# Loading k of the first nine pairs in whole rows and turning it by quarter products, with all operations in a new sequence

## The chip, the cores and the metric

The kernel runs on one core of a Trainium2 chip. A core has five engines that run side by side: TensorE (PE, matrix products), VectorE (DVE), ScalarE (ACT), GpSimd (POOL) and SyncE (SP, which here only issues DMAs). Sixteen DMA engines move data between HBM and the on-chip memory SBUF; PE writes its results to PSUM. The metric is the device time of one execution in microseconds (us); lower is better.

## The reference

All data is float32. Attention with normalised q and k on 8 batches x 12 heads, 448 tokens of 64 elements, is followed by a bilinear feed-forward block on the 3584 x 768 result, with 1536 inner columns.

```python
def rmsnorm(x, g):
    rms = np.sqrt(np.mean(x * x, axis=-1, keepdims=True) + 1e-06)
    return x / rms * g
q_n, k_n = (rmsnorm(q, g_q), rmsnorm(k, g_k))
scores = (1.0 / np.sqrt(64)) * np.matmul(q_n, k_n.transpose(0, 1, 3, 2))
attn = softmax(scores)
attn_out = np.matmul(attn, v)                       # (8, 12, 448, 64)
x = attn_out.transpose(0, 2, 1, 3).reshape(3584, 768)
out = ((x @ w_a) * (x @ w_b)) @ w_out
```

## The kernel before

**A pair.** The kernel treats four heads of one batch together: 24 such groups, which its code numbers p and which this text calls pairs, since each half of the 128 partitions holds two heads. Partitions 0 to 63 hold the first two heads, 64 to 127 the other two, and each partition holds 7 tokens of each of its heads (`NT` = 7).

**Loads.** q, k and v of a pair are 448 KB each, loaded by two DMAs on the SP queue (`loads`, L415). q and v are laid out so that each run in HBM is 7 tokens, 1,792 bytes. k is laid out with the two heads of a token side by side, so that each run is one token of one head, 256 bytes. For the very first pair the halves of q and k go by the SP and the ACT queue.

**Normalising.** ACT squares q and k (L462), DVE sums the squares (L464), POOL raises to the power -0.5 (L499). q is multiplied by its factor on DVE (L503), into a layout with the two heads of a token side by side; k isn't multiplied at all: its factor is the `scale` of the exponential, since the keys lie along the partitions of the scores (L594).

**Turning.** The products want q and k with the 64 elements of a head along the partitions. `turn_halves` (L525) turns a pair by 14 transposes on PE: for each of the 7 tokens and each half of the partitions, 64 rows x 128 columns against a 64 x 64 identity. ACT copies the result from PSUM (L548, L550). The first pair has its own copy of this in `turn_first`, between warm-up products that keep PE active.

**Attention.** For each of the 7 key blocks j of a pair there are four 64 x 64 x 448 score products (L588), two exponentials on ACT (L594), four value products (L610), and the sum over the keys: for the first four pairs by products with ones (L646), later by additions on DVE and POOL (L624) and one such product. The sums are inverted, spread by DMA and multiplied into the result (`invert`, `divide`). Scores, turned tiles and inverses share one PSUM tag, `sc`, with two buffers of two banks each.

**Weights.** At the same time the three weight matrices, which arrive as 64-bit floats, are rounded to float32 on DVE and ACT (`round_steps`, L247 to L256), combined into the factors of a fast matrix multiplication (L372), written back to HBM (`kept`), and streamed in again when they are used. Their loads of 768 KB a half and the writes go by the ACT queue (`hraw/n/h` and `lraw/n/h`: place n, half h).

**Feed-forward.** For two batches at a time there are first products (`quarter_products`, L1295; `deep_products`, L872) and last products (`last_product`, L996; `inner_products`, L1193). They begin while attention of later pairs is still running; up to about 225 us most of PE's work is attention, and attention of later pairs stands between feed-forward products after that.

**The order.** Every step is registered by `op(engine, us, key, emit, reads, writes, ...)` with a planned duration. `Plan.run` emits the 4,383 steps in the sequence that is stored, packed, in the string `ORDER`. Each engine then executes its own instructions in that sequence, and waits by semaphores for the data and the buffers of the others. `ORDER` alone decides what stands behind what; the durations in `op` are not used when the kernel is built.

```python
for w in range(2):
    pair = src[b, h0 + 2 * w:h0 + 2 * w + 2]
    nc.sync.dma_start(x[low_high[w]], pair.rearrange("h (p j) d -> p j h d" if nm == "k" else
                                                     "h (p j) d -> p h (j d)", j=NT))
...
nc.tensor.transpose(t[:, w, (j - j0) * D:(j - j0 + 1) * D], x[rows, j].rearrange("p h d -> p (h d)"), ident[rows, rows])
...
places = zlib.decompress(base64.b85decode(ORDER))
```

Of the kernel before, what the change touches and what calls it, by code (L numbers as in the profile page):

```python
# [12 lines left out]
FP32 = mybir.dt.float32  # L13
# [7 lines left out]
def _float_of(bits):  # L21
# [11 lines left out]
    "c-rkZ33OFOmba>2z4y1bzrW_^X9WZi2#d0afb@VOwk)Hl;0^%=5+ETV3JD;KU}OzzfUt>S6SF|r6PB<f5kWR-MYcw9qaDHNwx@ee-<JfTTYE-5"  # L33
    "<D8xztA4%r>ej8h)xEdw7dtU}6~u~YLMZWqYI@CpMNGpoOt0b(7{qAjRdnpCg1-egK!(^^o)~b03)}(cl;Gq5I3AtQrk|8;!dSy-k=3_FX7dNl"
    "jE8!{nfKGu(|Vp9K}MwZ0G13e2nNHzXP<*-pMmV0oXNX#VA8mWTfHkLY=+V|td*|=&o9Vdx(@y`bN%AXg@sV~1~?b2qzelmZ|Sn7B=65K5@ydD"
    "`G*nnVMgAZuVBWk+^e}uKZhlsuD+7H^3@fKSHiOM%Q(@O<ewEjIAeaW7S5=r3-eCGi8XZ2>#L!VxU1KY<$qpIVEM8?EZf_5@7HjB=e1qsuzmUg"
    "vg7KGt;V*Basj69DuqzVE+AW9K7+EA!YMd)@^~>EJ67Z@ehW6O1K7BB_XcstH+y&NfonT%FW<&V*;V*rJ3wg}S%F)Z7cJkk_2S!Sw{P=Qmz_C$"
    "x~%Nv;Z2nXkHOJ5;hjGo+51i9#yxxXUf;9lz=M0gtlWQf&wKkeR%|>`0p)LB{Al;?YB=0#{h^%)cOE#sVaNXc>-QhqcWB?ygOxEgl{NdS_nkis"
    "hqn7bEIVkF?XQGg@-EMwU2uIj?EGTK?>+;e<daWIoBXMyj9j_AWy_`Omo9C&^5vD^esS^h;)}(fd}^M*qMrZwf_(n+N3P2kN~KHZN<U-gzWDIN"
    "D<2mZfBb>^+m9}NbNSMx*rJQSDK2_%^Xapj&wWtzzFGAC`z7a#E_yB%U2v3~J$Lr#2Sr6kjvYT;bmGJ}CyyTg_oAAk*RCD;ebK)a)m#hzuI9^A"  # L40
    "XHI=qZGL*9>SR^%yN3@SK6?Jhx#RB~K6dnQO-<3M>i?)YRQ2xftE#K3e)H8=iPcr_)fClK7kzp{Ir!<pw<`7hZymjG0$|fID2K|8u=DiJ>XT4$"
    "ctyoKaHOLAdO4KuKGX!(9RR=+DuX?jYsxAvZYeqc(W=YmHm_3muPVXK%g+>-6a#U?_VrtrmTg#Dco5beT6=Kq7FYtGFW$Io$zoWy7>r8*^XHvg"
    "Na@@KbLYPYr`P2XI6env!K|4ubH>{axb|8u<i1L#PX~Zk046Iruw@clfC;V%<6%5xL-sg)7)I8ZEP%|6EK1YU(?_RMnl=guj7SAY84kmTnI?fD"
    "L$YDWU`l}ue2xG-^E5pD6g>4LJoN<9?%y9ChyIU3KX^p;JPduIZy)H>8=%)i@DLb10eZmwJ;;58bnk{rLDzfX-Y(FkGjt(_aW_B*Xy2|~2hx_@"
    "1#o8@fYz;`RZD1@1W7F{q}~*6Z%UdF()c!ebAv=kOn`)VNI=0O0MX%aI6|Xn=o}3NDS+R%9(-N^%LEg2T}J{shChHSCnpDTAbUbKj4Ob#OUH_1"
    "VeCsU6XTeWl{xk$@x_cW85zRpbPzCJ(JsPEFnsv%S94#5P1A>sXG2Axsi|2b(nqAF4jGY}vLrM0?a3J_DKH@|W%$Ao!(rawVZ#O|zmRMV88jFM"
    "4H`HBhUW|(n>-{r`MJTF$<GahLC@$<r#!0+8>a9%{P|e}h75R8?w>rM|6@;iwm<sh#77^0`0>a3Ir|NGq_4AY9~o`=i05HJ==Vb3K0@!_LhtUq"
    "9_rrx*Fw*3&paSW{hsL8PwLv$A@R<fcj?syI`!z%sZ;m+I(6&TrE{l_y*d_j?AYlZ;clTr_YU`U_*J)Gb?DZ$Lx(P1x^(E)`Cqzr?%c)Q{+{;5"
    "?skIaYUdK=QFn<BM@#X(=3?_^f^=^S-n0{M(vbs`SlhOY3D_Zt3X~ASY6m0|r~L)Ms67<4IEXm@1QZ0O5k_zH>&*L=5M^0G%1o0}%2e$PqcTHs"
    "*hFTCT;wq#uZ$MB5X*%?fH3A4m`S`AGwc*^cShDAJ5F_uSP?FS5f_mK!RP0K7cq&+bUL|?B~m7}VygBmHMI^JiVjg4vKTcjlTlqCcLVufkv`!D"  # L50
    "ZnEcL#I)Z5pC4(Ml$g4K(V!BrJ8BE4yw2imqu?V(V8KvOVE$%|d3|Un3v79HK~ah9`6CIt-QN)Mhp!2}CP{=T?CLm=fQ(4`sFd^+GGgRVl98H1"
    "&OA@Z3ull%9SqOHz-I<R)pJmF2o4;Cqm`#<B|Rio9o^gi$iDqGk5^RDYBXK{gP39;dAz|RpKPtzD(vRMmd(Pp507lyTw1od^u0c%rw$0ckN0`^"
    "UCuZ4dh^Y9Hg2ryCH(s9l9K)FcI<_s3bLWFCs|*zcIyLW7YbqZxgKkZ#Wia-t%g%;VCBkpw>j2seP{K`)hl0LxnkAw$`#8Gu2{Yf3f8SHcw>7("
    "VPRSKH!gQ8C94Q@UAbuWq7552EL*>>_rj%1dgmWmvaEDTe$~=d1#jik%EdH4zoKH^qTP!Z&Fc#DSHZlzy!Bg_u3NEe`Letvd2>!JUa~lU_1q<k"
    "7A;@2qNbqJvVvumuwX&{0+_#W{;q{H=WoAf9+bTXn`f8I&dpsg^X?gWuf8^S?wt8+U+*wGZ~EP{XHK7fctyd?yO&O*`7>$xjP`lcb6=S~dDhfU"
    "Q(h~5rFhDesne!SnmlQ0VPS_UbmHoct6rWsvE$V7ujEc?H)&e_<ViV`U(P9?H!*J#%bqZP{9O~qPtBp(lcsFUp1k4Z?1|Zh6S8x%?_9O&rLiks"
    "LXWv~OjcITm@(rPjUSgiu6*3MaWm%5p3!z@=8W7sGp4`Qdd!PilgEq^AZttpj7m?>O)vN;{l#hN`B|9@&y8*~|Lo{_X=$UzjvV=7){7&@jD%Ol"
    "W<u&{Ou8^JJtHkGJ$+BgsLZsK%(V23(Jj+zhF6b*W{?W0L!n8Np+lY@oG~~#Ic-#0@~Gsr5y`2kxRRQZGAOl4%D|!622Q&JQ{2Mrrt@#ZqNU-$"
    "CmK#1@N`2V^J#b@9TG<k7&%~g|6%=yCc?0Icp)L~`9Xsoj;DPYjXW7kAq?Tiq8`0JItoH02oUu5^grN7hi}ioYusrVos4?`OikB7#RyP6NuCxS"
    "k9xc3uG-uRs?#Z>Pewf4iJK(KIle4Vl?IA6M@dqB(Y~-@s#uh1c3oyErlzQk6%#8oElJZ=OH~Xdpdi4PWN5mMKYQvk_11=^D~6#271ghpdK>&S"  # L60
    "OhpZAilQ63ua&O&6(8=4G9rel>j7Q2n(J1SsR#YK?rnu2uVRD^O$n-oY50s5s%5FB8qou)r76A^hNdc-qG_tnr>m-_>Sl8#<X04>t%`J2#Ri4("
    "9W<5J$P<~F(a74T>rt&OpXD=j!wex`pVeA7{d$a1$4ynS0@W<7nWY#ZMGK(HN|NDI?7g_4`c|5%s<zbXX0{53)*59uBFGWh1vI;O^)*)_MwVqL"
    "5#5W3E&YbBgjLhjL)e3=sW&(9p{Qu8TG<q@(p2jaLIP+|%eJJYMJZ@It=7~nmF5QWS5?1VG`CTF8qxG<T~=fpL-r}M*OUXd%d)2V+gJuZHME&&"
    "XnsGcqG>I3*;J!cSqUp<$V^fUuW8AuEc+E%w(zaUs@~*nJy0#%`k)PyRM|k<NLsE{Pd0T~m(_@jy2+L-8_i?{g)~hzeP&BjAMI0RHH5}PbLlOK"
    "A*iZbSKW$$TwH$Q(VR|&Yuq8Z6N%x}Dfci@6&op{!{rb)Q4(cA;_`!{$R(Z2T!|$Ov_zuD$i(j<#N~ELnnWbQLs$bs;z?W_iH#*Z5{bkT5);9^"
    "9VF$UKwR5k=WvkvX=2N$=y0<@R3ID(#s>XyG(asPMWPHVK4{z#<fKW!AMkU(SB=DZ4a*97Rnrhqc81B{rxK5>Bzk1Gi9>NmC4}9E+anvqaw#so"
    "AtMeq@kq?$aJob$Nut*!d0pJ4aSfb_4H(|Cu}Tbg;6)}dPN;peVlflP1g9Xhvu|6014wvf;El^zD?(WV$wA{KDOM6&iP3UQOhAloFB0x2K{e?0"
    "JA77@6><>C%b1?Tn4uYx7IeyPh5(nt?O>`?a&YcW6kXh*q9I)(=ez-P36iJ^f-DFQy!9G!j)qo{B~v7KV~H~dHw;`u09Q~}hZ&CyMCRsNV;6Ty"
    "E{@yrl6NqN<Y*`fPQo}-P-cmX4MjIMIDSw}9}49f6&&`ZEJsV6y0Jc>tf4?T<%rI)5}~{i?z8V_g-X1!D7u|4&Z#8fT=1x>!_&ZFI9#Graymqm"
    "iJ~~1Q66z_r|!nog&j9bROEu2N^dwD+Qou{VIAV3RKn_{5i*kmB^MECQ$%!%q9jRzi1aCSGwPvk2i0RKRXH*i8*%Cs&}xbxaHp%^Z2~fNB2$qu"  # L70
    "50hMtBnj2#g2)6sL!{tDZgIAPD1wtZIBkfeMNU0+THS`#4T!p3z34<C=)#E>abdMURir9$;$cqal$ac0UvMWA8(oo@C^0lBMFrek^fVC7Q=*F!"
    "k;ojW2*j>67>{sLP9>Zm2Zk<SFHk4hh%V?7Xd+rxB}BICEDQoEo=BW4h{ZTZH%(v;DvAPk2~SanFo4w>j7At9&~OozN<<az$0OwEn7olFI$ciP"
    "wjxbp#6_Cd5w%^|L1|d@5Vw<<4zwB-o3%hwxCn8?6OusU;}c?HFc=*?j*!?G+!r8`kUu^?==1qnwD3iOcldpwCV?RFhW-91e=ryoxx?!V`(ymR"
    "C_l4&{@8e5j1`G^V=Sw46uZY~n*IQ>;z)vJ#bCF*x*0G7je?f!HMBUdnP3K@6HIC{B}yYvh8m=b;rA+*8Ba8~-xG~@j^<N>iHha5b1UX{J(Q#c"
    "v}T&p%&TZYs@*2UX?X9c_DvBoH5cYOOLgfk681SmYKY3j=i_dV*x2AMg9%!^lz`zA(n!D=#T`D@82zFlp1Ok8ry&|7B;Y233!|2?gct^(L`aB$"
    "1MgS|a06TdV4S&J0B+0%3`1YAGXU150tmI$soe<t!!`1~pFfQZ`GJgn)Y{)J{$wV0qdx|I3y{*AfZ9{7<%It{?7trNqjpN{K}hYR_6>G~*}oeD"
    ">`^-*b=Ws>Y2EHR2-Hn$G3&m`cWM6>i+UorF5PT@3!wGDdiHf(NWDT(&&UP|H}*oUgm6>BTS-IxraJj30J(MBw}i>JM!WeSH{j%!17zPl)bE4-"
    "X!ri-YV;=|&|6)Zeh(HpcYTA}QHMlpcimWn`pi}bruBHVo^pM>++3tLkiLc1%W;#}Up4qUaC(y&+z<<Ha;CS+@U1BHzqAScyIw-R3nV|qzsOJZ"
    "Q9}M3Wb#u&f&4)E$j==`KUZ9me^kMKY5!~q_WxxgKU*M?UxM<N_J2NC(Eo*aBmcv3@-s!(FG2fD`{C^`Cf^JG"
# [68 lines left out]
def kernel(  # L148
# [126 lines left out]
    def fast_body(ld, wk, ps_s, ps_o, ps_mm, dram):  # L275
# [8 lines left out]
        TURN = 0.42  # L284
# [130 lines left out]
        def loads(p, nm):  # L415
# [4 lines left out]
            def emit():  # L420
                x = ld.tile([P, NT, 2, D] if nm == "k" else [P, 2, NT * D], FP32, tag=nm, name=nm + "_sb", bufs=2 if nm == "v" else 1)
                for w in range(2):
                    pair = src[b, h0 + 2 * w:h0 + 2 * w + 2]
                    nc.sync.dma_start(x[low_high[w]], pair.rearrange("h (p j) d -> p j h d" if nm == "k" else
                                                                     "h (p j) d -> p h (j d)", j=NT))
                xs[nm, p] = x
            if p == 0 and nm != "v":
                def begin():
                    xs[nm, p] = ld.tile([P, NT, 2, D] if nm == "k" else [P, 2, NT * D], FP32, tag=nm, name=nm + "_sb", bufs=1)

                def half(w):
                    pair = src[b, h0 + 2 * w:h0 + 2 * w + 2]
                    queue[("SP", "ACT")[w]].dma_start(
                        xs[nm, p][low_high[w]], pair.rearrange("h (p j) d -> p j h d" if nm == "k" else "h (p j) d -> p h (j d)", j=NT))
# [4 lines left out]
            op("SP", 1.28 if nm != "k" else 1.4, p - (1.8 if nm == "v" else 2.0), emit, [f"firsts{PREP}"] if p >= HELD else [], [t], new=[t],  # L439
               kb={"q": 620, "k": 800, "v": 530}[nm], dmas=2)  # L440
# [4 lines left out]
        def normalize(p):  # L445
# [8 lines left out]
            def squares(s, nm):  # L454
                sq = tile_of(f"sq{nm}{p}", "sq", 1)

                def square():
                    x = xs[nm, p]
                    t = xs["sq", nm, p] = wk.tile([P, 2 * NT, D], FP32, tag="sq", name="sq")
                    flat = (x.rearrange("p h (j d) -> p (h j) d", d=D) if nm == "q" else  # L460
# [61 lines left out]
            qn = tile_of(f"qn{p}", "qn", 1)  # L522
            op("DVE", 1.15, key, apply, [f"{ms}/q", f"q{p}"], [qn], new=[qn], lock=True)

        def turn_halves(t, x, j0, j1):  # L525

            for j in range(j0, j1):
                for w in range(2):
# [1045 lines left out]
```

## Time and profile before

| | before |
|---|---|
| time, median of 3 runs | 1473.81 us |
| lowest and highest run | 1473.35 and 1478.22 us |
| profiled execution, its time | 1477.19 us |
| profiled execution, its span | 1475.2 us |
| PE busy | 1452.8 us, 98% of the span |
| DVE busy | 998.3 us, 68% |
| ACT busy | 438.1 us, 30% |
| POOL busy | 332.6 us, 23% |
| DMA packets | 188,884, of them under 512 bytes 62,564 |

The profile is of one execution, which took its own time; the median is of other executions. The span goes from the first to the last instruction. In the rows of a profile, L530 is line 530 of the kernel, PE is a product, PEld the load of a product's stationary operand, and names such as `pt<-ident,k_sb` are the tiles written and read. A row in square brackets names the idle time of the engine before the instruction and what ended it. "SPq" and "ACTq" are the instructions that issue DMAs. In the windows view the columns are the window, its length, busy time (and instructions) of PE, PEld, DVE, ACT and POOL, the granted share of the TensorE clock, the mean busy share of the DMA engines, and GB/s.

### The profile page before, as it was taken

The page shows a single profiled execution, that of the slowest core. Times are in us where ns is not written, and L with a number is a line of the kernel's source. Part 1 is how long each engine was busy: PE and PEld are TensorE (multiplying, and loading weights), DVE is VectorE, ACT ScalarE, POOL GpSimd, SP SyncE. Part 2 cuts the span into 40 slices and gives each one's busy share as a digit, 9 for nine tenths or more (in the row PEclk, how much of TensorE's full clock was granted, in tenths as well). Part 3 has the DMA queues.
Part 4 walks back from the last instruction along what each step waited for, and adds up shares of the span by engine and source line. Part 5 has one row for each costly group of instructions (what it writes and reads, how often), then busy time and mean ns, then how long its engine had stood idle before and what let it go on. Part 6 is the DMA issues. An engine that isn't in the chain of part 4 may idle for free.

```text
span 1475.2 us, 21710 instructions
## 1 busy us (share of the span) xinstructions
PE 1452.8 (98%) x8222; PEld 944.5 (64%) x8222; DVE 998.3 (68%) x1575; ACT 438.1 (30%) x792; POOL 332.6 (23%) x175
## 2 busy tenths in 40 slices
PE   7999999999999999999999999999999999999998
PEld 5433434555444555555544445799997899999898
DVE  4998699888675233344668776466677676666785
ACT  5887752111554000000257770011111011111100
POOL 3456632102233001110255650011210001121000
PEclk9999999999999999999999999999999999999999
DMA  8876467554442555556555635555554755555355
GB/s 222 243 232 173 128 170 224 187 175 170 140 124 82 166 162 168 185 150 179 170 161 143 153 99 169 174 159 154 165 156 162 268 180 169 150 165 175 129 190 152
DMA packets 188884, 248.02 MB, mean 168 GB/s; under 512 B 62564, under 2 KB 161380, under 8 KB 182116
## 3 DMA queue, kind: packets, MB, share of 16 engines
q1 hardware_dynamic: 159652, 192.61, 45.3%
q10 hardware_dynamic: 29120, 53.94, 10.8%
q8 instruction: 67, 1.10, 0.3%
q14 instruction: 45, 0.37, 0.1%
HBM read 188.35 MB, written 57.93 MB: 167 GB/s over the span
## 4 chain that ended last, share of the span: by engine, by line
PE 87%; DVE 5%; DMA 3%; ACT 2%; issue 1%; SPq 0%; POOL 0%; ACTq 0%; DVEq 0%
PE pq L1295 24%; PE dg L872 17%; PE po L996 17%; PE sc L588 6%; PE o L610 6%; PE da L872 6%; PE a L1193 2%; PE g L1193 2%; DMA k_sb<-in_k_dram 1%; PE su L646 1%; PE pt L530 1%; PE b L1193 1%; PE e L1193 1%; PE d L1193 1%; DMA q_sb<-in_q_dram 1%
## 5 line engine op out<-in xcount | busy, mean ns | idle before, releaser
L1295 PE MATMUL pq<-x,st 128*128 128x448 f32 x1008 | 385.1, 541 | 3.3 <-DVE hT L1348 1.3
L1295 PEld LDWEIGHTS pq<-x,st 128*128 128x128 f32 x1008 | 189.5, 190 | 192.8 <-issue 174.4
L594 ACT ACTIVATE ET<-sc,ms 128x448 f32<-128x448 f32 x336 | 191.5, 638 | 88.8 <-PE sc L588 65.9
L499 POOL TENSOR_TENSOR ms<-ms,expo 128x14 f32<-128x14 f32 x47 | 146.6, 3120 | 104.1 <-DVE ms L497 95.0
L872 PE MATMUL dg<-dT,st 128*128 128x224 f32 x672 | 166.5, 353 | 0.1
L872 PE MATMUL dg<-x,st 128*128 128x224 f32 x672 | 164.8, 354 | 0.9 <-DVE dF L919 0.9
L996 PE MATMUL po<-st,hT 128*128 128x384 f32 x492 | 164.1, 488 | 0.0
L588 PE MATMUL sc<-qkT 64*64 64x448 f32 x1344 | 154.1, 545 | 3.4 <-ACT ET L594 2.1
L610 PE MATMUL o<-ET,v_sb 64*64 64x448 f32 x1344 | 149.7, 541 | 0.0
L900 POOL TENSOR_TENSOR hT<-dF 128x448 f32<-128x448 f32 x42 | 47.3, 1139 | 428.1 <-DVE dF L895 428.1
L996 PEld LDWEIGHTS po<-st,hT 128*128 128x128 f32 x492 | 92.4, 190 | 66.9 <-issue 6.5
L872 PEld LDWEIGHTS dg<-x,st 128*128 128x128 f32 x672 | 126.1, 190 | 4.3 <-DVE dF L919 3.6
L872 PEld LDWEIGHTS dg<-dT,st 128*128 128x128 f32 x672 | 126.3, 190 | 2.2 <-DVE dt L912 1.1
L624 POOL TENSOR_TENSOR sum<-sum,ET 128x896 f32<-128x896 f32 x40 | 90.2, 2254 | 131.8 <-DVE sum L624 70.0
L872 PE MATMUL da<-x,st 128*128 128x224 f32 x504 | 117.8, 353 | 0.0
L588 PEld LDWEIGHTS sc<-qkT 64*64 64x64 f32 x1344 | 46.0, 132 | 86.5 <-issue 41.3
L610 PEld LDWEIGHTS o<-ET,v_sb 64*64 64x64 f32 x1344 | 50.3, 133 | 72.8 <-issue 65.3
L872 PEld LDWEIGHTS da<-x,st 128*128 128x128 f32 x504 | 94.8, 190 | 0.7
L895 DVE TENSOR_TENSOR dF<-dF 128x896 f32<-128x896 f32 x84 | 92.0, 1098 | 3.2 <-DVE dF L924 0.5
L996 PE MATMUL po<-st,fin 128*128 128x384 f32 x252 | 86.2, 491 | 0.0
L885 ACT COPY dt<-da 128x224 f32<-128x224 f32 x84 | 29.1, 347 | 191.3 <-PE da L872 148.1
L1343 POOL TENSOR_TENSOR hT<-hT,t 128x448 f32<-128x448 f32 x12 | 16.6, 1382 | 292.8 <-DVE t L1341 265.5
(147 smaller groups left out, 1700.0 us busy)
## 6 DMA issues: line engine op xcount, KB each, us to landing
st<-kept_o SPq DMA_DIRECT2D x28, 1152.0 KB
st<-kept_s SPq DMA_DIRECT2D x84, 320.0 KB
kept<-st ACTq DMA_DIRECT2D x12, 1344.0 KB
st<-kept SPq DMA_DIRECT2D x12, 1344.0 KB
st<-kept SPq DMA_DIRECT2D x84, 192.0 KB
ti<-kept_t SPq DMA_DIRECT2D x48, 288.0 KB
kept_s<-ds SPq DMA_DIRECT2D x30, 448.0 KB
v_sb<-in_v_dram SPq DMA_DIRECT2D x48, 224.0 KB
```

Source lines behind the costliest of these rows:

```text
L499: lambda: nc.gpsimd.tensor_tensor(msf(), msf(), expo[:, 0:2 * NT * (b - a)], ALU.pow), [], names)
L588: nc.tensor.matmul(t[low_high[w], e, 0:S], lhsT=qkTs[p][low_high[e], 1, w * S + j * D:w * S + (j + 1) * D], rhs=qkTs[p][low_high[e], 0, w ...
L594: nc.scalar.activation(E[:, e], scs[p, j][:, e, 0:S], AF.Exp, scale=rs[p][:, 1, 2 * j + e:2 * j + e + 1])
L610: nc.tensor.matmul(os_[p][low_high[e], w, 0:S], lhsT=xs["v", p][low_high[w], e, j * D:(j + 1) * D], rhs=ETs[p, j][low_high[w], e], start=( ...
L624: two[e].tensor_tensor(sums[p], sums[p] if j > 1 else ETs[p, 0], ETs[p, j], ALU.add)
L872: nc.tensor.matmul(to(), lhsT=W(w), rhs=t(), start=not more and k == 0, stop=k == len(terms) - 1, skip_group_check=True)
L885: nc.scalar.copy(part(0), a())
L895: take("DVE", 1.09, lambda: V.tensor_tensor(F[to], F[to], F[other], ALU.add), allF(other), allF(to), lock=True)
L900: lambda: two[e].tensor_tensor(C(i, n), F[g][:, 0:S], F[g][:, S:2 * S], ALU.mult), allF(g),
L996: nc.tensor.matmul(held["po"][:, 0:HALF], lhsT=a[0]()[:, c], rhs=sts[beta, 12 + place_of[f]][:, c], start=(c == 0), stop=(c == MH - 1))
L1193: nc.tensor.matmul(held[bank], lhsT=x()[:, c], rhs=y(c), start=(start and c == 0), stop=(stop and c == MI - 1), skip_group_check=True)
L1295: nc.tensor.matmul(banks[bank][:, 0:S], lhsT=sts[at][:, f, c * P:(c + 1) * P], rhs=quads[x][:, c], start=(start and c == 0), stop=(stop an ...
```

## The change

A new constant `WHOLE` = 9. For the pairs 0 to 8, k is loaded in the layout of q (runs of 1,792 bytes) and turned by `quarter_turns`: 28 plain products of 64 x 64 x 64 with the identity, one for each token, half and head, in place of 14 transposes. The squares and the scale of the exponential address k's factors in the new layout. The pairs 9 to 23 keep the old form. The planned durations are changed (they had their part in making the new string), and `ORDER` is another string of the same length in steps: all steps stand in a new sequence.

```diff
 ORDER = (
-    "c-rkZ33OFOmba>2z4y1bzrW_^X9WZi2#d0afb@VOwk)Hl;0^%=5+ETV3JD;KU}OzzfUt>S6SF|r6PB<f5kWR-MYcw9qaDHNwx@ee-<JfTTYE-5"
+    "c-rk)2Y6LgwqCoOcJDp?+?Jc%BqSs>69~l;X#x()d=CY2q^PJ=fg2!=mI8?d2`xw<0Ya!5g8^<x0tf^`PXI;whysFxql}+C+nYBtzVGdugyQ&p"
...
-        TURN = 0.42
+        TURN, WHOLE = 0.45, 9
...
             def emit():
-                x = ld.tile([P, NT, 2, D] if nm == "k" else [P, 2, NT * D], FP32, tag=nm, name=nm + "_sb", bufs=2 if nm == "v" else 1)
+                mixed = nm == "k" and p >= WHOLE
+                x = ld.tile([P, NT, 2, D] if mixed else [P, 2, NT * D], FP32, tag=nm, name=nm + "_sb", bufs=2 if nm == "v" else 1)
                 for w in range(2):
                     pair = src[b, h0 + 2 * w:h0 + 2 * w + 2]
-                    nc.sync.dma_start(x[low_high[w]], pair.rearrange("h (p j) d -> p j h d" if nm == "k" else
+                    nc.sync.dma_start(x[low_high[w]], pair.rearrange("h (p j) d -> p j h d" if mixed else
                                                                      "h (p j) d -> p h (j d)", j=NT))
...
-                flat = (x.rearrange("p h (j d) -> p (h j) d", d=D) if nm == "q" else
+                flat = (x.rearrange("p h (j d) -> p (h j) d", d=D) if nm == "q" or p < WHOLE else
                         x.rearrange("p j h d -> p (j h) d"))
...
+        def quarter_turns(t, x):
+
+            for j in range(NT):
+                for w in range(2):
+                    rows = low_high[w]
+                    for h in range(2):
+                        nc.tensor.matmul(t[low_high[h], w, j * D:(j + 1) * D], lhsT=x[rows, h, j * D:(j + 1) * D], rhs=ident[rows, rows],
+                                         start=True, stop=True)
...
-                    turn_halves(t, xs["k", p] if n == 1 else qns[p], 0, NT)
+                    if n == 1 and p < WHOLE:
+                        quarter_turns(t, xs["k", p])
+                    else:
+                        turn_halves(t, xs["k", p] if n == 1 else qns[p], 0, NT)
...
-                op("PE", TURN, key, turn, [f"{nm}{p}" if n else f"qn{p}", f"half{p - 1}"], [pt], new=[pt], mode="half")
+                whole = n == 1 and p < WHOLE
+                op("PE", 0.83 if whole else TURN, key, turn, [f"{nm}{p}" if n else f"qn{p}", f"half{p - 1}"], [pt], new=[pt],
+                   mode="quad" if whole else "half")
...
+            at = (lambda e: e * NT + j) if p < WHOLE else (lambda e: 2 * j + e)
...
                     nc.scalar.activation(E[:, e], scs[p, j][:, e, 0:S], AF.Exp,
-                                         scale=rs[p][:, 1, 2 * j + e:2 * j + e + 1])
+                                         scale=rs[p][:, 1, at(e):at(e) + 1])
```

The same is done for the first pair in `turn_first`. The order of instructions that the new string gives, beside the old: PE keeps 618 of its 1455 steps in their place and moves none by more than 12 places; ACT moves none by more than 10, SP by 14, DVE by 26, POOL by 2. Around the second pair, k1, the queues stand as follows.

```
before  SP:  q1, v0, k1, v1, q2, k2
        ACT: ... first two exponential pairs, load hraw/1/1, third pair, squares of q1, load hraw/1/0, two pairs, squares of k1, two pairs
after   SP:  q1, v0, k1, v1, q2, k2
        ACT: ... first three exponential pairs, load hraw/1/1, squares of q1, one pair, load hraw/1/0, one pair, squares of k1, two pairs
```

## The prediction

> **What bounds the kernel now.** I read the page first, then the waits of TensorE in the first 50 us, the timeline around the longest of them, and a table of busy time by stretches.
>
> ```profile
> span 1475.2 us, 21710 instructions
> PE 1452.8 (98%) x8222; PEld 944.5 (64%) x8222; DVE 998.3 (68%) x1575; ACT 438.1 (30%) x792; POOL 332.6 (23%) x175
> PE   7999999999999999999999999999999999999998
> ...
> PE 87%; DVE 5%; DMA 3%; ACT 2%; issue 1%; SPq 0%; POOL 0%; ACTq 0%; DVEq 0%
> ```
>
> TensorE (PE) is busy for 98% and is 87% of the chain that ended last. So a saving elsewhere is worth only the PE idle time that it ends, and every PE microsecond added on a full stretch is paid whole. Idle PE is 22.4 us in all; 6.4 of them are the last stores after the last product (1468.8 to 1475.2). What can be won lies at the start:
>
> ```profile
> PE pt L530 <- ACT ET L594: 3.8, 1, 3.8
> PE warm L409 <- POOL ident masks.py:199: 1.4, 1, 1.4
> PE pt L530 <- DMA k_sb<-in_k_dram: 1.2, 1, 1.2
> PE pt L530 <- DVE qn L503: 0.8, 2, 0.5
> PE sc L588 <- ACT ET L594: 0.6, 1, 0.6
> ```
>
> The largest wait, 3.8 us, names ScalarE (ACT), but the timeline shows what ACT itself stood at:
>
> ```profile
> 23.19 1.16 ACT L594 ACTIVATE ET<-sc,ms 128x448 f32<-128x448 f32 x2 [0.40 <-PE o L610]
> ...
> 26.71 0.15 PEld L646 LDWEIGHTS su<-ET,ones 64*64 64x64 f32 x4 [0.22 <-issue]
> 29.37 0.95 ACT L462 ACTIVATE sq<-k_sb 128x896 f32<-128x896 f32 x1 [5.02 <-DMA k_sb<-in_k_dram]
> 30.23 2.19 ACT L594 ACTIVATE ET<-sc,ms 128x448 f32<-128x448 f32 x4
> 30.36 1.09 DVE L464 TENSOR_REDUCE ms<-sq 128x14 f32<-128x896 f32 x1 [5.94 <-ACT sq L462]
> 31.42 0.65 PE L530 MATMUL pt<-ident,k_sb 64*128 64x64 f32 x14 [3.78 <-ACT ET L594]
> ...
> 32.59 1.01 PE L530 MATMUL pt<-ident,qn 64*128 64x64 f32 x14 [0.51 <-DVE qn L503]
> ```
>
> The squares of the second pair's k wait 5.02 us for its load (issued at 14.44, landed at 29.37). Queued behind them on ACT are four exponentials of pair 0, and PE's next work needs the banks that these free. VectorE (DVE) starves too. The stretches show what follows:
>
> ```profile
> 25.00:30.00 5.00, 2.64 (x30) 0.77 (x20) 0.00 (x0) 0.63 (x1) 1.87 (x1) 1.00 0.57 164
> 30.00:35.00 5.00, 3.06 (x36) 1.91 (x40) 4.64 (x6) 4.59 (x8) 0.73 (x1) 0.73 0.72 213
> 35.00:40.00 5.00, 5.00 (x56) 1.89 (x52) 4.86 (x6) 3.18 (x5) 2.29 (x1) 0.92 1.17 262
> ...
> 50.00:100.00 50.00, 49.59 (x546) 19.32 (x546) 47.12 (x58) 41.66 (x64) 21.48 (x7) 1.00 0.89 259
> ```
>
> [...]After the gap the granted clock is 0.73 and 0.92 of full: 5 x 0.27 + 5 x 0.08 = 1.75 us of PE lost on top. From 50 to 100 us PE has 0.4 us idle, DVE is 94% busy and the DMA engines 89%: three resources nearly full at once.
>
> **The change, part by part.** *Loads.* A k load of 448 KB is now 1,792 runs of 256 bytes; in the first nine pairs it becomes 256 runs of 1,792 bytes, the form of q. The trace's packet records of the first 100 us give a median of 25 ns for 256 bytes and 94 ns for 1,792: 1792 x 25 / 16 = 2.8 us of all 16 engines against 256 x 94 / 16 = 1.5. That saves 1.3 us a load where DMA is full. It shortens the time only where PE waits for a load.
>
> Pair 0: q has landed at 5.59 and k at 8.15, 2.56 us later; at 1.5 it would be there at about 7.1. PE ends its warm-up products at 6.94, so most of its 1.2 us wait goes. The end of this stage, though, hangs on the normalised q (DVE, 10.43 to 11.6), which stood behind the reduction of k's squares (9.20 to 10.29). With k 1.1 us earlier that reduction and two small DVE operations that the new sequence puts behind it (0.2 and 0.14 us) end by about 9.9, so q starts some 0.6 us earlier and the first scores at about 14.4 and not 14.97. The first k turn's longer time lies beside this. **-0.6.**
>
> Pair 1: ACT reaches the squares at 24.35 (23.19 + 1.16). To end the whole stall k must land 9.9 us after its issue, not 14.9. The q load of the same pair, in long runs on the same queue through the same crowd of weight loads, was issued at 11.67 and used from 20.32: 8.65 us. The new sequence helps: v of pair 1 and k stand ahead of the weight half hraw/1/1 (768 KB), which moves behind one more pair of exponentials on ACT (1.16 us). So I let k land at about 23: the 3.78 us gap goes, with it the 0.51 us before q's turn (DVE and POOL were held up by the same load), and the clock's 1.75 us. **-6.0.**
>
> [...]
>
> *Quarter turns.* A k turn was 14 transposes of 64x128. Its slot is 0.58 us (8.15 to 8.73) with a change of tile shape, and such a change costs 0.15 (attention products follow each other every 0.75 us, every 0.91 before another shape): 0.42 bare. It becomes 28 products of 64x64, two instructions each. Attention products in the same four quarters stream 448 columns per instruction in 0.375 us, four at a time: 64 columns take 0.054, and 56 / 4 = 14 waves make 0.75 us. The plan's own entry is 0.83. I take +0.4 a turn. Eight turns lie on a full PE (pairs 1 to 8): **+3.3** (0.41 each).
>
> [...] But the rows of four 64x64 weight loads, each 132 ns long, end within 0.15 us, so starts in different quarters are only some 6 ns apart. [...]
>
> *The rest.* The exponentials read their scale from another place, the squares another layout: same count, same shape, 0. The number of DMA instructions on SP and ACT stays. POOL keeps its order but for neighbours.
>
> *The new sequence.* Of 1455 PE steps 618 keep their place; none moves over 12 places, DVE's none over 26, ACT's 10, SP's 14. Shape changes on PE fall from 132 to 130: -0.3. k's and q's turns stood back to back and q's then waited (0.32 us at 49.20, 0.20 at 64.76); now one to five products stand between: -0.5. At 108 to 112 us PE waits 0.58 and 0.28 between scores; a value product now stands among them: -0.5. **-1.3.** The remaining waits up to 224 us (some 7 us in pieces of 0.2 to 1.0, most behind DVE) are shuffled; I let them stay alike, with 3 us to either side. At 200 to 225 us DVE is busy 24.1 of 25, so PE arriving earlier is worth something only if DVE does too; it does, since its own 5.94 us of starving goes with the same load. After 224 us the products of the feed-forward part run without gaps (four waits over 0.3 us in 1250), and loads are still issued several products ahead. 0, with 2 us to either side.
>
> **Sum.** -0.6 - 6.0 + 3.3 - 1.3 = -4.6 us. The profiled execution took 1477.19 us (span 1475.2 and 2.0 around it), which is 3.4 above the median of the runs, 1473.81 (1473.35 to 1478.22). Taken from the median: 1469.2. A measurement of this kernel can tell about 0.3% (4.4 us) from no change, so the forecast is just beyond it.
>
> **The rivals.** *The stall belongs to the profiled execution.* Runs lie at 1473.4, 1473.8 and 1478.2; if the load of k was late only there and in the highest run, the median has little to give: about -2 at the start, -1.3, +3.3: 1473.8. For it: the profiled time is near the highest run. Against it: 256-byte runs are long in every execution.
>
> *The turn is bound by instructions (slower).* The half turn's 14 loads and 14 products pass in 0.42 us, 15 ns each. If PE takes 112 instructions at that pace, a turn is 1.7 us, +1.26 over eight turns +10.1, and the sum is +2.2; if the start then gives 4.2 and not 6.0, +4, at 1478. It ends above zero from an added 1.0 us a turn. For it: nothing in the trace shows 64-column products in quarters. Against it: the four loads within 0.15 us.
>
> *The new sequence costs.* DVE, at 94%, or an SP load moved back (k of pair 15 and q of pair 15 change places by 5 and 7) brings new waits of 8 us or more: 1477 to 1480.
>
> *The load comes as late as before*, held by its slowest engine behind the weights: near -0.6 - 1.3 + 3.3 = +1.4, 1475.
>
> **How the numbers follow.** The stall goes and the rest is as costed: 0.64, of which 0.52 beyond 0.3% faster and 0.12 within, where 1462.5 is its lower end (the shuffled waits give 3 us and later stages 2 more). The stall is the profiled execution's own, or it stays: 0.10, within 0.3%. The turns bound by instructions: 0.14; the sequence costs: 0.12; both slower. The range goes up to 1479, which takes in the middle of the slower cases.
>
> **What would show it.** Right: no PE gap over 1 us between 20 and 36 us; granted clock 1.00 there; the squares of k not waiting over 1 us; the quarter turn's slot at 0.75 to 0.85 us; PE idle up to 225 us down by about 7 us. Wrong: k still landing after 25 us, a turn at 1.4 us or more, or new waits for DVE or DMA between 36 and 225 us that add up to over 5 us.

## The result, and the profile after

| | before | after |
|---|---|---|
| median of 7 runs each | 1475.02 us | 1468.41 us |
| lowest and highest run | 1473.35 and 1480.18 us | 1467.58 and 1469.76 us |
| profiled execution, its time | 1477.19 us | 1468.41 us |
| profiled execution, its span | 1475.2 us | 1466.5 us |

The ratio is 0.9959, with a 95% interval from 0.9946 to 0.9973: about 0.4% faster, clear of the noise but not by much. The forecast was 1469.2, which is 4.6 us less. Against this set of runs of the kernel before, the difference is 6.6 us, against the three later sets 4.8 to 5.9. The total came out; how it was composed did not, as the experiments show.

The page of the changed kernel:

```profile
span 1466.5 us, 22464 instructions
PE 1451.9 (99%) x8600; PEld 949.1 (65%) x8600; DVE 997.1 (68%) x1575; ACT 438.2 (30%) x792; POOL 333.0 (23%) x175
PE   9999999999999999999999999999999999999998
...
PE 95%; DVE 3%; ACT 1%; issue 1%; DMA 0%; POOL 0%; DVEq 0%; ACTq 0%; POOLq 0%
```

PE's busy time is within 1 us of what it was (1452.8), although it executes 378 more product instructions (nine times 56 in place of 14). The first of the 40 slices went from 7 tenths to 9, and TensorE's share of the chain that ended last rose from 87 to 95%. Here are PE's waits in the first 50 us, and then the second pair's turns and what led to them in the timeline:

```profile
PE warm L409 <- POOL ident masks.py:199: 1.4, 1, 1.4
PE sc L606 <- ACT ET L614: 0.6, 1, 0.6
```

```profile
7.48 1.04 PE L532 MATMUL pt<-ident,k_sb 64*64 64x64 f32 x56
8.45 0.60 PE L409 MATMUL warm<-ident 128*128 128x128 f32 x3
...
23.53 0.95 ACT L463 ACTIVATE sq<-k_sb 128x896 f32<-128x896 f32 x1
24.51 1.09 DVE L465 TENSOR_REDUCE ms<-sq 128x14 f32<-128x896 f32 x1 [1.57 <-ACT sq L463]
...
25.93 1.00 PE L532 MATMUL pt<-ident,k_sb 64*64 64x64 f32 x56
...
27.62 0.59 PE L540 MATMUL pt<-ident,qn 64*128 64x64 f32 x12
```

The waits of 3.8, 1.2 and 0.8 us are gone. The squares of the second k stand at 23.53 with no wait in brackets, and its turn at 25.93, 5.5 us earlier than in the profile of before. The same stretches as in the prediction:

```profile
25.00:30.00 5.00, 5.00 (x110) 2.51 (x106) 4.89 (x7) 4.48 (x7) 3.84 (x2) 1.00 0.99 363
30.00:35.00 5.00, 5.00 (x56) 2.09 (x52) 4.79 (x6) 4.24 (x8) 0.00 (x0) 1.00 1.06 283
...
50.00:100.00 50.00, 50.00 (x682) 21.51 (x675) 47.25 (x56) 42.43 (x68) 24.56 (x8) 1.00 0.85 255
```

PE is full and its clock whole in each. Read only against the one profile of before, this looks like the forecast come true step by step. Whether the time came from there is another question: the change has two parts, and the profile of before is one execution.

### The profile page after: what moved, and what is told of

The parts are those of the page before. It is cut to its first block, busy times and chain, and to the rows that moved or that the text cites. A ratio compares the mean times of both kernels' runs of the same rounds, so it can differ in the third digit from the quotient of the medians.

```text
span 1466.5 us, 22464 instructions
## 1 busy us (share of the span) xinstructions
PE 1451.9 (99%) x8600; PEld 949.1 (65%) x8600; DVE 997.1 (68%) x1575; ACT 438.2 (30%) x792; POOL 333.0 (23%) x175
## 4 chain that ended last, share of the span: by engine, by line
PE 95%; DVE 3%; ACT 1%; issue 1%; DMA 0%; POOL 0%; DVEq 0%; ACTq 0%; POOLq 0%
PE pq L1315 24%; PE dg L892 17%; PE po L1016 17%; PE sc L606 8%; PE o L630 8%; PE da L892 6%; PE su L666 3%; PE a L1213 2%; PE g L1213 2%; PE pt L540 1%; PE e L1213 1%; PE b L1213 1%; PE d L1213 1%; PE warm L409 1%; PE pt L532 0%
## 5 line engine op out<-in xcount | busy, mean ns | idle before, releaser
L644 DVE TENSOR_TENSOR sum<-sum,ET 128x896 f32<-128x896 f32 x60 | 66.4, 1107 | 30.7 <-POOL sum L644 22.5
```

The lines of the kernel that those rows point to most:

```text
L644: two[e].tensor_tensor(sums[p], sums[p] if j > 1 else ETs[p, 0], ETs[p, j], ALU.add)
```

## The experiments

The runs shared three sets of runs of the kernel before, whose medians were 1473.22 us (28 runs from 1471.21 to 1481.37), 1474.29 (23 runs from 1470.93 to 1478.65) and 1473.5 (23 runs from 1471.4 to 1480.29). Ratios are to the set that was measured together with the run.

### Which part carries the gain

**whole_old_order**: the changed loads and turns, in the old sequence.

```diff
 # the changed kernel
-ORDER = ( ... the new sequence ... )
+ORDER = ( ... the sequence of before ... )
```

> The changed loads and quarter turns, in the old sequence. Theory 1 (the late load of the second pair's k is what costs, and the long runs end it; the sequence gives 1 to 4 us): no TensorE wait over 1 us near 25 to 32 us, time 3 us under the kernel before, about 1472. Theory 2 (the sequence frees the start, by putting loads ahead of the weight half hraw/1/1): the wait of over 2 us stays, and the time is the kernel before plus the turns' 3 us, about 1477.

Measured: 1472.54 us (12 runs from 1471.88 to 1473.98), ratio 0.9993 [0.9982, 1.0004]. Theory 1's time (1472) and its missing wait came out: PE waits at most 0.6 us between 1.4 and 50 us in this profile. But the kernel before took 1473.22 in the same set, so the 3 us under it did not.

**halves_new_order**: the other half of the change: k in runs of 256 bytes and half turns as before, in the new sequence.

```diff
 # the kernel before
-ORDER = ( ... the sequence of before ... )
+ORDER = ( ... the new sequence ... )
```

> The old loads of 256-byte runs and half turns for all pairs, in the new sequence. Theory 1: the second pair's k still lands after 25 us and TensorE waits over 1.5 us for what stands behind its squares; 9 turns are shorter by 0.4 us (-3.6), but the shape changes on TensorE rise from 130 to 144 (14 x 0.155 = +2.2): about 1470 to 1474, above the changed kernel. Theory 2: the wait is gone, and the time is 1.4 us under the changed kernel, about 1467.

Measured: 1468.04 us (11 runs from 1467.3 to 1468.69), ratio 0.9959 [0.9946, 0.9971]. That is 1.0 above theory 2's number and below all of theory 1's. The squares of the second k start at 23.75 us in its profile, with no wait, though k comes in 256-byte runs.

The four kernels make a square:

| median, us | old sequence | new sequence |
|---|---|---|
| k in 256-byte runs | 1473.2 to 1475.0 (before) | 1468.04 |
| k in whole rows | 1472.54 | 1468.41 |

The new sequence alone is worth as much as the whole change. The loads and turns alone cannot be told from no change.

**before_again** and **before_third** are the kernel before, unchanged, profiled once more each.

> The kernel before once more, for a second profile. If the late k is in every execution: again a wait of over 2 us near 27 to 32 us. If the halved clock after it is a matter of where the gap falls: the wait may stand there with the clock at 1.00, and the time is then nearer 1474 than 1477.

> The kernel before, a third profile: either the late k with its wait of some 4 us and a time of 1476 or more, or no wait over 0.6 us before 50 us and 1472 to 1473.

They took 1472.68 us (span 1470.7) and 1472.76 us (span 1470.8). The timeline of before_again around the place where the first profile had its 3.78 us gap, and PE's waits in its first 50 us:

```profile
24.32 0.95 ACT L462 ACTIVATE sq<-k_sb 128x896 f32<-128x896 f32 x1
...
27.65 0.52 PE L530 MATMUL pt<-ident,k_sb 64*128 64x64 f32 x10
```

```profile
PE warm L409 <- POOL ident masks.py:199: 1.4, 1, 1.4
PE sc L588 <- ACT ET L594: 0.6, 1, 0.6
```

The same program, and the second k is there in time: the squares wait for nothing. The first profile's largest wait belonged to that execution. Even there it was not worth 6.0 us: the last product ends 4.7 us later than in before_again (1468.80 against 1464.13), as of the 5.6 us lost up to 225 us, 1.0 is won back between 532 and 957 us (table below).

The runs show how often something of the kind happens. Each has a mean granted clock, 0.998 in the profiled execution and 0.999 in the two new ones. In the three sets, all 14 runs over 1475.5 us have 0.998 or less. The 46 of 74 runs with more lie between 1470.93 and 1475.46, with a median of 1472.7, near the two new profiles. So the upper runs are those that lost clock; at which wait, the runs do not say.

The waits of before_third, up to 60 us, are others again:

```profile
PE pt L530 <- DMA k_sb<-in_k_dram: 1.6, 1, 1.6
PE pt L530 <- DVE qn L503: 1.5, 1, 1.5
```

These stand at 6.66 us (k of the first pair) and at 43.26 (the q turn of the third pair), and the second pair has no such wait: neither of the two outcomes expected. Nor is either a late k. The turn of the first k starts at 8.15, 8.23 and 8.25 us in the three profiles; what differs is when the warm-up products ahead of it end (6.94, 8.10 and 6.66). And the q turn waits for DVE, which had waited for a small copy of the sums (`few<-rec`, 3.5 KB) that stands ahead of the normalising of q:

```profile
43.35 0.25 DVE L696 RECIPROCAL few<-few 112x16 f32<-112x16 f32 x1 [1.57 <-DMA few<-rec]
43.55 1.09 DVE L503 TENSOR_TENSOR qn<-q_sb,ms 128x896 f32<-128x896 f32 x1
```

**whole2_new_order**: the changed kernel with whole rows for two pairs instead of nine.

```diff
-        TURN, WHOLE = 0.45, 9
+        TURN, WHOLE = 0.45, 2
```

> Long runs and quarter turns for the first two pairs only, new sequence. If the long runs matter at the start alone: seven turns shorter by 0.4 (-2.8), 12 more shape changes (+1.9), so about 1 us under the changed kernel, 1467.5. If the long runs also carry the stage of 36 to 130 us, where the DMA engines are 85% busy: new waits for k there and a time above the changed kernel, 1470 or more.

Measured: 1470.06 us (12 runs from 1468.07 to 1472.2), ratio 0.9973 [0.9961, 0.9986]. Seven fewer quarter turns did not make it faster; the 1467.5 expected was missed by 2.6 us. Shape changes can be counted. A half turn works in another tile shape (`64*128`) than the attention products around it (`64*64`), and a quarter turn in the same one. In the new sequence, in which products stand between k's turn and q's, PE changes shape 144 times with halves only, 142 times here, and 130 times with nine pairs in whole rows; in the old sequence, 132 with halves and 130 with whole rows. A change costs about 0.155 us, an estimate midway between two differences in the traces of before and after: an attention step takes 0.75 us ahead of its like and 0.86 ahead of another shape, a feed-forward step 1.94 us ahead of its like and 2.13 ahead of attention. The 12 more here come to 1.9 us, against the 7 x 0.40 = 2.8 us that the shorter turns save, so 0.9 us should be left as a gain. Something else shows in the windows view, by its clock column (the last but two):

```profile
207.24:210.65 3.41, 1.36 (x13) 0.56 (x10) 3.41 (x3) 0.00 (x0) 0.91 (x1) 1.00 0.73 89
210.65:214.06 3.41, 3.41 (x6) 1.40 (x5) 3.38 (x4) 0.00 (x0) 2.16 (x1) 0.50 0.00 0
```

PE waits 2.05 us for DVE in the first row, and in the second the granted clock is 0.50, which by an estimate costs 0.5 x 3.41 = 1.7 us (the 8 product instructions from 210.35 us on are busy 4.97 us; 12 like them are busy 4.78 at 371.73 in the changed kernel). In the changed kernel two waits for the same DVE lines, 1.1 and 1.4 us, stand there without a loss of clock. With the lost time as it is counted below, this stage (150 to 225 us) takes 1.0 us more (5.2 against 4.2), and the last product ends 0.9 us later than in the changed kernel. But this is one execution, and at 1469.07 us it is 1.0 below the median of its own kernel. The runs do not bear the clock out as the cause: the five with a mean clock of 0.998 or less have a median of 1469.99, the other seven 1470.13. Why this kernel is 1.6 us above the changed one and 2.0 above halves_new_order stays open.

### Where in the sequence

For these readings each of PE's 1455 steps was matched between kernels. The time from the start of one step to that of the next, less its planned duration, less 0.155 us where the tile shape changes, is called lost time below; it contains waits, late starts and clock losses. A half turn counts as 0.42 us and a quarter turn as 0.82 in all columns. Stages are by time, so a step near an edge can stand on either side.

| us from start | before, profile shown | before_again | whole_old_order | halves_new_order | after |
|---|---|---|---|---|---|
| 0 to 225 | 24.6 | 19.0 | 16.3 | 14.9 | 13.1 |
| 225 to 532 | 1.9 | 1.9 | 1.8 | 1.1 | 1.1 |
| 532 to 957 | 1.9 | 2.9 | 2.9 | 1.7 | 1.7 |
| 957 to 1214 | 2.7 | 2.7 | 2.7 | 1.3 | 1.3 |
| 1214 to the last product | 1.0 | 1.0 | 1.0 | 2.6 | 2.6 |
| all | 32.0 | 27.4 | 24.7 | 21.6 | 19.8 |
| shape changes | 132 | 132 | 130 | 144 | 130 |
| last product ends | 1468.80 | 1464.13 | 1464.76 | 1460.25 | 1459.89 |

From before_again to after, lost time falls by 7.6 us, the nine longer turns add 9 x 0.40 = 3.6, and two shape changes less give 0.3: 4.3, and the last product ends 4.24 earlier. No single wait carries it. One that went and two that came show the kind. First, PE's waits from 360 to 400 us in before_again:

```profile
PE pq L1295 <- DVE U L1325: 1.0, 1, 1.0
```

The same place in the timeline of the changed kernel, and its waits from 1300 us on:

```profile
371.73 4.78 PE L1315 MATMUL pq<-x,st 128*128 128x448 f32 x12
376.44 0.98 PE L606 MATMUL sc<-qkT 64*64 64x448 f32 x8
```

```profile
PE dg L892 <- DVE dF L939: 1.0, 2, 0.6
```

Before, a feed-forward product at 375.54 waited 1.02 us for DVE, behind a row of attention products. In the new sequence 12 product instructions of the feed-forward stand there and the attention follows, with no wait. Two waits for DVE, of 0.62 us at 1312.5 and 0.42 at 1353.0, are new; two for the same line of DVE, of 0.56 us at 1088.8 and 0.33 at 1105.9 in before_again, are gone.

**early_new** and **late_new**: the changed kernel with one sequence up to PE step 240 (about 225 us) and the other after it. early_new has the new one first, late_new the old one first.

```diff
 # early_new
-ORDER = ( ... the new sequence ... )
+ORDER = ( ... the new sequence to PE step 240, the old one from there ... )
 # late_new
+ORDER = ( ... the old sequence to PE step 240, the new one from there ... )
```

> Changed loads and turns; new sequence up to TensorE step 240 (about 225 us), old sequence after it. If the sequence's gain is a sum of separate waits, as the two profiles' stretches add up (stretches up to step 240: 3.3 us shorter than with the old sequence): 1472.5 - 3.3 = 1469.2. If the gain is made late alone (the gain of the early part is given back later): 1472.5.

> Changed loads and turns; old sequence up to TensorE step 240, new sequence after it. Separate waits: the stretches after step 240 are 1.5 us shorter, 1471.0. If the early part carries all: 1472.5.

Measured: early_new 1469.29 us (7 runs from 1468.51 to 1470.09), ratio 0.9974 [0.9963, 0.9985]; late_new 1471.9 us (11 runs from 1470.9 to 1474.29), ratio 0.9986 [0.9975, 0.9996]. Against whole_old_order, 1472.54, the early part is worth 3.3 us and the late part 0.6. Together that is 3.9, and the whole new sequence gives 4.1. early_new came out as expected (1469.2), late_new 0.9 above (1471.0). The sums had taken differences of profiles from a median: whole_old_order's profiled execution took 1473.49 us, 0.95 above its median. Profile against profile, late_new's last product ends 1.6 us earlier, as the stretches gave.

**best_of_both**: stretches between two places at which both sequences have issued the same steps can be exchanged. The new sequence loses time in four: PE steps 268 to 282 (0.29 us), 532 to 650 (0.40), 1214 to 1294 (1.12) and 1312 to the end (1.11). This kernel takes the old sequence in those.

```diff
-ORDER = ( ... the new sequence ... )
+ORDER = ( ... the new sequence, with the old one in PE steps 268-282, 532-650, 1214-1294, 1312-1454 ... )
```

> The changed kernel with the old sequence in the four stretches in which the new one is slower by the profiles (TensorE steps 268 to 282, 532 to 650, 1214 to 1294 and from 1312 on: 0.29, 0.40, 1.12 and 1.11 us). Separate waits: 1468.4 - 2.9 = 1465.5, faster than both. If a wait removed only moves to the next stretch: 1468.

Measured: 1465.84 us (5 runs from 1465.09 to 1466.32), ratio 0.9947 [0.9934, 0.9961]. The four differences, 2.9 us taken from 1468.4, give 1465.5, and 1465.84 is within 0.4 of it. It is 2.6 us below the changed kernel's median, and its slowest run is below the changed kernel's fastest, though in another set of runs; the two ratios to the kernel before have intervals that overlap. early_new, in the same set, is 3.45 above it. So the new sequence is better in sum and worse in places.

### What a quarter turn costs

**turns_twice**: the changed kernel with the quarter turns of pairs 1 to 8 executed twice into the same tile.

```diff
                     if n == 1 and p < WHOLE:
                         quarter_turns(t, xs["k", p])
+                        quarter_turns(t, xs["k", p])
```

> The changed kernel with every quarter turn of pairs 1 to 8 done twice (a repetition of the same products). If TensorE alone bounds the stage up to 160 us, as the prediction costed it: 8 x 0.75 = +6.0, 1474.4. If VectorE and ScalarE bound it as much, the longer turns take the place of waits: +2 to +4, 1470.5 to 1472.5.

Measured: 1476.59 us (11 runs from 1474.84 to 1477.63), ratio 1.002 [1.0011, 1.0029]: 8.2 us above the changed kernel. Two doubled turns in the timeline, those of the second pair and of a later one:

```profile
26.16 1.57 PE L532 MATMUL pt<-ident,k_sb 64*64 64x64 f32 x92
28.46 0.51 PE L532 MATMUL pt<-ident,k_sb 64*64 64x64 f32 x18 [0.73 <-issue]
...
59.53 1.81 PE L532 MATMUL pt<-ident,k_sb 64*64 64x64 f32 x112
```

From the start of a turn to that of the next step, six slots went from 0.82 to 1.63 us. That of pair 7, 1.27 us in the changed kernel, became 1.79, so 0.3 us of it took the place of a late start; and in the second pair the slot took 1.82 us more, with a wait that the profile puts down to issue. 6 x 0.81 + 0.52 + 1.82 = 7.2 of the 8.2 us; a wait for DVE at 216 us that is 0.6 longer is most of the rest. That is more than the 6.0 of turns that only take their time on PE, and far from the 2 to 4 of turns that are partly hidden: next to nothing hides a turn.

**halves_together**: if the quarter turn is that dear, half turns in its place should gain, as long as they add no shape changes. From best_of_both, whole rows for two pairs only, and the k turns of pairs 2 to 8 as half turns directly ahead of the q turns, their copies on ACT with them (129 shape changes, as in best_of_both).

```diff
 # best_of_both
-        TURN, WHOLE = 0.45, 9
+        TURN, WHOLE = 0.45, 2
-ORDER = ( ... that of best_of_both ... )
+ORDER = ( ... the same, with the k turns of pairs 2 to 8 moved to just ahead of the q turns ... )
```

> The best mix of the two sequences, with long runs and quarter turns for pairs 0 and 1 alone; the k turns of pairs 2 to 8 are half turns again and stand directly before their q turns, so that shape changes do not rise. If a turn's 0.4 us is paid in full and nothing else: 1465.8 - 7 x 0.4 = 1463.0. If q's turn then waits for k's copy and the banks, as it did in the kernel before: 1465 to 1467.

Measured: 1470.57 us (12 runs from 1469.29 to 1472.54), ratio 0.9976 [0.9965, 0.9988]. A miss: 4.7 us above best_of_both (measured in another set) instead of below it. PE's waits from 40 to 225 us, first of this kernel, then those of best_of_both that answer to them:

```profile
PE pt L539 <- ACT qkT L560: 3.0, 3, 1.0
PE pq L1314 <- DVE t L1355: 2.1, 1, 2.1
PE pq L1314 <- DVE t L1371: 1.4, 1, 1.4
```

```profile
PE pq L1314 <- DVE t L1371: 1.4, 1, 1.4
PE pq L1314 <- DVE t L1355: 1.1, 1, 1.1
PE pt L539 <- ACT ET L613: 0.8, 2, 0.5
```

And one of the three in the timeline:

```profile
45.92 0.65 PE L539 MATMUL pt<-ident,k_sb 64*128 64x64 f32 x14
46.61 0.91 ACT L560 COPY qkT<-pt 128x896 f32<-128x896 f32 x1 [1.50 <-PE pt L539]
47.57 0.65 PE L539 MATMUL pt<-ident,qn 64*128 64x64 f32 x14 [1.00 <-ACT qkT L560]
```

The q turn needs the PSUM buffer that the k turn filled, and waits for ACT to copy it out (0.91 us). Three of seven pairs pay 1.0 us each. Stretch by stretch against best_of_both's profile, those three pairs cost 3.3 us, the wait for DVE that went from 1.1 to 2.1 us another 1.0, and the last product ends 4.2 us later. With attention products between the two turns, as in the new sequence, the copy runs beside them. A half turn there takes 0.58 us, the step ahead of it 0.11 more and the step behind it 0.05 more, 0.74 in all; the quarter turn in its place takes 0.82 and adds nothing to its neighbours. So the tile shape pays back most of the longer turn, and no more: halves_new_order, without any quarter turn, is as fast as the changed kernel. What counts is the work between the turns. Half turns in best_of_both's own sequence were not run.

### What makes loads late

**hraw_later**: the kernel before, with the one step that the prediction held responsible moved: the load of the weight half hraw/1/1 is issued behind the third pair of exponentials.

```diff
 # ACT's queue, kernel before
-two exponential pairs, load hraw/1/1, third pair
+three exponential pairs, load hraw/1/1
```

> The kernel before (256-byte runs, half turns, old sequence) with one step moved: the load of the weight half hraw/1/1 is issued on ScalarE's queue after the third pair of exponentials and not before it, some 1.2 us later. If the late k of the profiled execution comes from sharing the DMA engines with that load: all runs within 2 us of 1472.5, none above 1475, while the kernel before keeps runs up to 1478 and more. If not: a spread as the kernel before has.

Measured: 1474.35 us (12 runs from 1470.9 to 1477.16), ratio 1.0002 [0.999, 1.0014]. The theory falls: the runs spread over 6 us. In its own profile the second k is in time (squares at 24.48 us), as in two of the three of the kernel before, and the two long waits, at 6.55 and 44.51 us, are those of before_third: the first k behind warm-up products that end early, and q behind the small copy of the sums, for which DVE waits 2.3 us.

```profile
PE pt L529 <- DVE qn L502: 1.9, 1, 1.9
PE pt L529 <- DMA k_sb<-in_k_dram: 1.9, 1, 1.9
```

## Why the prediction was right in its total and wrong in its reasons

**The start of pair 0, -0.6: about right.** The first scores start at 14.54 us after (14.28 in whole_old_order) and at 14.97, 15.04 and 15.06 in the three profiles of before, which is 0.4 to 0.8 us.

**The stall of pair 1, -6.0: the step that was wrong for the time that counts.** In the profile it came out: the gap of 3.78 us, the 0.51 ahead of the q turn and the clock loss are gone. But the prediction summed against one execution (1477.19) and then took the sum from the median of the others (1473.81). It had named the rival that says so, "the stall belongs to the profiled execution", and gave it little. before_again and before_third have no such stall, and whole_old_order, which has all of the new loads, does not lower the median measurably. The prediction's argument against that rival, that 256-byte runs are long in every execution, does not bear on it: in before_again k comes in the same runs, and its squares start at 24.32 us without a wait.

What the loads did bring is smaller. In the old sequence lost time falls by 2.7 us (27.4 to 24.7), all of it before 150 us. That pays for most of the turns' 3.6. The 1.3 us of DMA a load were too many: in the changed kernel, where k comes in that size too, packets of 1,792 bytes took a median of 125 ns in the first 100 us, not 94, so 256 x 125 / 16 = 2.0 us and a saving of 0.8. And the upper runs went: 7 and 12 runs with whole rows in nine pairs lie within 2.2 us (late_new's 11 within 3.4), those of before within 8 to 10. The new sequence without whole rows has no such upper runs either (11 within 1.4 us), so the runs cannot credit that to the loads. Why the second k came late in the first profile, and what the upper runs wait for, is open; the load of hraw/1/1 alone isn't the reason for the spread.

**Quarter turns, +3.3: right in size.** The slot is 0.82 us bare against 0.42, so 0.40 each, and turns_twice shows a turn paid almost in full. In the old sequence, where q's half turn follows, k's slot goes from 0.48 to 0.92 and the slot ahead of it from 0.86 to 0.75: 0.33 each, 2.6 for eight. 56 instructions in 0.82 us are 14.6 ns each: in the turn at 41.20 us of the changed kernel's trace they start in fours, 6 or 7 ns apart, with about 58 ns from one four to the next. The prediction had worked out some 6 ns from the weight loads of before. No run shows the 1.4 us a turn that stands among its signs; in its place stand the 0.82, and the rival with 1.7 us a turn is out as well. What the sum lacked is the other side: that a turn in the shape of its neighbours may stand between them. In the new sequence, whole rows save 14 shape changes, 2.2 us; the prediction saw 132 become 130 and booked -0.3.

**The new sequence, -1.3: the term that was mis-sized.** With whole rows in both, lost time falls from 24.7 to 19.8: -4.9 between two profiles (-4.1 between the medians), of which 3.2 up to 225 us and 1.7 after it. The separated turns (-0.5) and the scores at 108 to 112 us (-0.5) were booked, the second too high: the wait of 0.58 us there is still in the changed kernel, at 103.28, and only the 0.28 went. (Between the turns of pairs 1 to 8 stand none to four steps, not one to five.) The "7 us in pieces of 0.2 to 1.0" were set at 0 with 3 us to either side, and the later stages at 0 with 2. Both came out on the gaining side, inside the ends given. So, in medians, loads and turns came to -0.7 where the sum had -3.3, with an interval that takes in 0, and the sequence to -4.1 where it had -1.3: the total agrees because the two errors cancel, which is luck.

**The clock.** The prediction booked 1.75 us for it within the 6.0. In the trace of before the clock was 0.50 for 3.41 us, from 32.35 us on, behind the gap of 3.78 us: eight product instructions of the sums, which take 0.75 us at full clock, took 1.55 there (33.52 to 35.07). The 4.2 us that one rival takes for the start is about the 6.0 without those 1.75; no run shows such a gap without the loss of clock. The last section shows which gaps were followed by half clock.

**The rivals.** The first was right for the stall and wrong in its sum (1473.8), as it took the sequence at -1.3. The new sequence does cost in places, 2.9 us in the four stretches exchanged in best_of_both, far from the 8 us of the rival. No load comes late in the profile after.

**The signs given in advance** (no gap over 1 us between 20 and 36 us, whole clock, squares not waiting, a slot of 0.75 to 0.85 us) all came out, PE's idle time up to 225 us with them: 13.9 us in the first profile of before, 6.5 after. They could not show the error: each compares with the one profile that had the stall. In before_again that idle time is 8.4.

## What to carry to other kernels

Before a wait in a profile is priced, ask whether the median execution has it: if the profiled execution is 3.4 us above the median and the wait is 3.8 us long, take a second profile, or price the wait at what the spread of the runs allows. When a change comes with a new sequence, run the two apart, since a sequence can gain in many waits of a few tenths what no single row shows. Stretches of two sequences can be combined; here they added up as computed to within 0.9 us. Put work between two steps that share one buffer (without it, three turns waited 1.0 us each in halves_together), and count what a step of another tile shape costs among them (here about 0.155 us a change). A wait names the last engine in a row of waits: follow it back, here from q's turn over DVE to a copy of 3.5 KB.

## What the hardware showed beyond that

**Short gaps and the clock.** A gap of 2.05 us in whole2_new_order was followed by 3.41 us at half clock, one of 2.06 us in halves_together by none. What differs is where they fall. In all 13 traces each stretch of one granted clock, but for the last, which the end of the trace cuts off, lasts a whole multiple of 3.413 us (27.31, 3.41 and 1437.01 in before, 1457.49 in after, 204.8 and 3.41 in whole2_new_order), so each trace can be cut into windows of that length. In whole2_new_order the gap lies inside one window (the two rows shown above). In halves_together it is split between two, 1.62 and 0.44 us:

```profile
207.18:210.59 3.41, 3.09 (x24) 1.56 (x20) 3.41 (x6) 1.66 (x3) 0.76 (x1) 1.00 1.10 257
210.59:214.00 3.41, 1.79 (x17) 0.47 (x16) 3.41 (x2) 0.70 (x2) 1.64 (x1) 1.00 1.00 134
214.00:217.41 3.41, 2.97 (x8) 1.63 (x9) 3.41 (x4) 0.00 (x0) 1.43 (x1) 1.00 0.00 0
```

The gap of 3.78 us in the first profile left PE idle for 1.3 us in one window and 2.76 in the next (with part of the wait behind it), and 3.41 us at half clock followed that one. Over all 13 traces, a window with 2.05 us of idle PE or more was followed by half clock, and a window with 1.93 or less (the end of whole_old_order; 1.65 at most before the last product) was not. No window lies between; 2.05 us is 60% of a window. The windows count from where the clock's record begins, at 5.04 us in before and at 6.32 in after.

**Small products in quarters.** 28 products of 64 x 64 x 64, 56 instructions, took 0.82 us beside others of the same shape, and 0.97 (7.48 to 8.45) ahead of another shape, here full tiles of 128 x 128.
